# Sketched linear attention and a SwiGLU layer: per-head sums carried to every quadrant by on-chip copies, and a bank counter set

## The chip, the cores and the metric

The kernel runs on one core of a Trainium2 chip. Times are device microseconds. The time before is 309.65 us, the median of three runs (309.54 to 311.03); the profiled execution has a span of 307.8 us from its first to its last instruction. TensorE is called PE here, its weight loads PEld, VectorE DVE, ScalarE ACT, GpSimd POOL, and SP is the engine whose queue issues most of the transfers.

## The reference

Two layers follow each other. All of it is float32 in the kernel; the inputs arrive as 64-bit floats, and the weights are narrowed on the chip.

```python
def phi(x):                                   # x: batch 4, heads 4, tokens 1088, 32
    a = einsum('rd,bhsd->bhsr', S1, x)        # r = 8 sketches
    b = einsum('rd,bhsd->bhsr', S2, x)
    return einsum('bhsi,bhsj->bhsij', a, b)   # 64 features
q_p, k_p = phi(q), phi(k)
kv  = einsum('bhsf,bhsd->bhfd', k_p, v)       # 64 x 32 for each head
z   = sum(k_p, axis=s)                        # 64 for each head
num = einsum('bhsf,bhfd->bhsd', q_p, kv)
den = einsum('bhsf,bhf->bhs', q_p, z) + 1e-06
x   = (num / den) as (4352 tokens, 128)
g   = x @ w_gate                              # 128 -> 1536
out = (silu(g) * (x @ w_val)) @ w_out         # 1536 -> 128
```

## The kernel before, in words

The 4352 tokens are four batches of 1088. A batch is cut into three blocks of 384, 384 and 320 tokens. A **unit** (`unit`, L633) is one block with one of the 12 slices of 128 hidden columns: a matmul with `wg`, one with `wv` (both at L641), a Silu on ACT (L647), and a product on DVE into `hj` (L657). A **down** (`down`, L665) is the matmul of one such `hj` with `wo` into the block's accumulator (L671), run two units later. So for each block and slice PE does three wide matmuls, and these are most of the work. Each fp32 matmul leaves two records in the trace.

The first batch's attention runs by itself at the start, with its own scheme (L755 to L836). The attention of batches 1 to 3 is a generator (`attention`, L476): after every unit from the eighteenth (`z >= 17`) of the first batch on, the loop calls `next(att)` once, and the generator emits a few instructions and yields. What lies between two yields is therefore queued on the engines between two units. [...] a long DVE instruction of the generator stands in front of the next `hj`.

The steps of the generator for one batch are: transposes of K and Q (four steps); the sketches of all tokens, `key_products` for K and again for Q (L278, 18 matmuls each, weights of 128 x 64, into the wide PSUM tiles `a` and `b`); the K features `phk` on DVE; the sum of `phk` over its chunks on POOL (`feature_sums`, L465, tile `zs`); two empty steps; then `kvz`: `key_values` (L312, 36 matmuls of 128 x 32 weights) and the ones-matmul (L523, 128 x 128 weights, 256 columns) that sums `zs` over the partitions and spreads it to all of them; ACT copies `kvs` and `zrep` out (L527, L531); one step later two matmuls with the identity (L537) turn `kvs` to the other layout, and ACT copies it to `kvr` (L542). After that DVE forms `phq` (L553), reduces it (L560), divides (L569 to L575), forms the Q features and transposes them (L301, L584), and 32 matmuls of 32 x 32 (L597) give the numerators, which ACT and DVE copy to `xT` (L614).

The kernel uses eight banks of PSUM. The wide tiles `a` and `b` take four; `g0`, `g1`, `g2` and `acc` are single banks. `bank()` without a name takes `free_banks[turn[0] % len(free_banks)]` and adds one to the counter. In the first 17 units of the main list four banks rotate. At `z == 17` `acc` is taken out of the rotation, because the downs begin and need it, and three rotate from then on (L854). `down` takes `g0` by name for the accumulator of block 1 and `acc` for every other one (L670). `turn[0]` is set to 2 at L816; from there one unit and four more before the loop, and 17 in it, take two banks each, so the counter stands at 2 + 10 + 34 = 46 at `z == 17`.

Of the kernel before, what the change touches and what calls it, by code (L numbers as in the profile page):

```python
# [19 lines left out]
def kernel(  # L20
# [73 lines left out]
    def wide(tag):  # L94
        return psum.tile([P, 2, TB], FP32, tag=tag, name=tag)
# [70 lines left out]

    rebias = const.tile([P, 1], FP32, name="rebias")
    ident = const.tile([P, P], FP32, name="ident")
    ones = const.tile([P, P], FP32, name="ones")
    own = const.tile([P, H], FP32, name="own")  # L170
    sel = const.tile([P, Dh], FP32, name="sel")
    warm = nc.const_aps.tensor(1.0, [P, TB], mybir.dt.bfloat16)
# [83 lines left out]

    xT = const.tile([P, NT], FP32, name="xT")

    s12 = const.tile([P, H, 2, R], FP32, name="s12")
    sq = const.tile([P, 2, R, R], FP32, name="sq")  # L260
    def turn_k(c0, c1):
        four = "p (a c) d -> p a c d"
# [8 lines left out]
            in_=qld[:, 2 * x0 : 2 * x0 + 2 * n, :],  # L271
        )

    def key_products(ps, c0, c1, src=kT):

        for c in range(c0, c1):
            for a in (0, 2):
                nc.tensor.matmul(  # L278
                    ps[32 * a : 32 * a + 64, 64 * (c - c0) : 64 * (c - c0) + 64],
                    src[:, c, a : a + 2, :].rearrange("p a t -> p (a t)"),  # L280
                    s12[:].rearrange("p h t r -> p (h t r)"),
                    start=True,
                    stop=True,
                )
# [13 lines left out]
    def key_features(phk, prod, c0, c1, engine=nc.vector):  # L298
        ka, kb = prod
        n = (c1 - c0) * H  # L300
        engine.tensor_tensor(  # L301
            out=phk[:, c0:c1, :, :, :].rearrange("p c h i j -> p (c h) i j"),
            in0=ka.unsqueeze(3).to_broadcast([P, n, R, R]),
            in1=kb.unsqueeze(2).to_broadcast([P, n, R, R]),
            op=ALU.mult,
        )
# [13 lines left out]
    def unit_sums(kz, phk, c0, c1, order):  # L320

        for c in range(c0, c1):
            a = c % 4
            same = [x for x in order if x % 4 == a]
            nc.tensor.matmul(  # L325
                kz[32 * a : 32 * a + 32, 0 : H * F],
                ones[:, 0:Dh],
                phk[:, c, :, :, :].rearrange("p h i j -> p (h i j)"),
                start=(c == same[0]),
                stop=(c == same[-1]),  # L330
            )
# [144 lines left out]
    def attention(b, qsteps):  # L476
# [13 lines left out]
                load_q(b + 1)  # L490
            yield
        kp, qp = wide("a"), wide("b")
        for ps, src in ((kp, kT), (qp, qT[:].rearrange("p (c a) t -> p c a t", a=4))):
            for i, c in enumerate(kpieces):
                key_products(ps[:, i, :], *c, src=src)
        ka = apool.tile([P, NC * H, R], FP32, tag="kas", name="kas")
        qab = apool.tile([P, 2, NC * H, R], FP32, tag="qab", name="qab")

# [7 lines left out]
        for n, (i, c0, c1) in enumerate(((0, 0, 3), (0, 3, 5), (1, 5, 7), (1, 7, 9))):  # L506
# [10 lines left out]
        zs = feature_sums(phk)  # L517
        yield
        yield
        yield  # L520
        kvz = wide("a")
        key_values(kvz[:, 0, :], phk, 0, NC)
        nc.tensor.matmul(kvz[:, 1, 0 : H * F], ones[:], zs, start=True, stop=True)  # L523

        kvs = apool.tile([P, 2, 4, 32], FP32, tag="kvs", name="kvs")
        zrep = apool.tile([P, H * R, R], FP32, tag="zrep", name="zrep")
        nc.scalar.copy(  # L527
            kvs[:],
            kvz[:, 0, 0:F].rearrange("p (g f) -> p g f", g=2).unsqueeze(2).to_broadcast([P, 2, 4, 32]),
        )  # L530
        nc.scalar.copy(zrep[:], kvz[:, 1, 0 : H * F].rearrange("p (x r) -> p x r", r=R))  # L531
        if b + 1 < B:
            load_v(b + 1, [nc.sync] * 4)
        yield
        kvp = wide("b")[:, 0, 0 : 2 * P].rearrange("p (g n) -> p g n", g=2)
        for g in range(2):
            nc.tensor.matmul(  # L537
                kvp[:, g, :], kvs[:, g, :, :].rearrange("p a f -> p (a f)"), ident[:],
                start=True, stop=True,
            )  # L540
        kvr = apool.tile([P, 2, P], FP32, tag="kvr", name="kvr")
        nc.scalar.copy(kvr[:], kvp)  # L542
        phq = apool.tile([P, NC, H, R, R], FP32, tag="phqs", name="phq")
        phT = apool.tile([P, H, 2, NC, 32], FP32, tag="phk", name="phT")
        dot = apool.tile([P, NC * H, R], FP32, tag="dot", name="dot")
# [1 line left out]
        for s0, s1 in qsteps:  # L547
            thirds = [c for c in fpieces if s0 <= c[0] < s1]
            for c0, c1 in thirds:
                n, x = c1 - c0, slice(H * c0, H * c1)  # L550
                prod = phq[:, c0:c1, :, :, :].rearrange("p c h i j -> p c (h i) j")
                fac = qab[:, 0, x, :].rearrange("p (c h) i -> p c (h i)", h=H)
                nc.vector.tensor_tensor(  # L553
                    out=prod,
                    in0=zrep[:].unsqueeze(1).to_broadcast([P, n, H * R, R]),
                    in1=fac.unsqueeze(3).to_broadcast([P, n, H * R, R]),
                    op=ALU.mult,
                )
                yield
                nc.vector.tensor_reduce(  # L560
                    out=dot[:, x, :],
                    in_=phq[:, c0:c1, :, :, :].rearrange("p c h i j -> p (c h) j i"),
                    axis=AX.X,
                    op=ALU.add,
                )
                yield
            x = slice(H * s0, H * s1)
            w = H * (s1 - s0)
            nc.vector.tensor_tensor(  # L569
                out=dot[:, x, :], in0=dot[:, x, :], in1=qab[:, 1, x, :], op=ALU.mult  # L570
            )
            nc.vector.tensor_reduce(out=den[:, x], in_=dot[:, x, :], axis=AX.X, op=ALU.add)
            nc.vector.tensor_scalar_add(den[:, x], den[:, x], 1e-6)
            nc.vector.reciprocal(den[:, x], den[:, x])
            nc.vector.tensor_tensor(  # L575
                out=qab[:, 0, x, :], in0=qab[:, 0, x, :],
                in1=den[:, x].unsqueeze(2).to_broadcast([P, w, R]), op=ALU.mult,
            )
            yield
            for c0, c1 in thirds:  # L580
                x = slice(H * c0, H * c1)
                key_features(phq, (qab[:, 0, x, :], qab[:, 1, x, :]), c0, c1)
                yield
                nc.vector.transpose(  # L584
                    out=phT[:, :, :, c0:c1, :].rearrange("p h g c t -> p c (h g) t"),
                    in_=phq[:, c0:c1, :, :, :].rearrange(
                        "p c h (g i) j -> p c (h g) (i j)", g=2
                    ),
                )
                yield  # L590
            num = wide("a"), wide("b")
            for g in range(2):
                for h in range(H):
                    for a in range(4):
                        r = slice(32 * a, 32 * a + 32)
                        n = min(s1, (NX - a + 3) // 4) - s0
                        nc.tensor.matmul(  # L597
                            num[a // 2][32 * h : 32 * h + 32, a % 2, 0 : 32 * n],
                            kvr[r, g, 32 * h : 32 * h + 32],
                            phT[r, h, g, s0 : s0 + n, :],  # L600
                            start=(g == 0),
                            stop=(g == 1),
                        )
            for u, engine in enumerate((nc.scalar.copy, nc.vector.tensor_copy)):
                for c0, c1 in query_runs(s0, s1):
                    if c1 == NC and u == 1:
                        continue
                    t0 = S * b + P * c0
                    wd = 4 if c1 < NC else 2
                    dst = xT[:, t0 : t0 + 32 * wd * (c1 - c0)].rearrange(  # L610
                        "p (c a t) -> p a c t", a=wd, t=32
                    )
                    src = num[u][:, :, 32 * (c0 - s0) : 32 * (c1 - s0)]
                    engine(  # L614
                        dst[:, 2 * u : 2 * u + 2], src.rearrange("p a (c t) -> p a c t", t=32)
                    )
            yield
# [111 lines left out]
    for h in range(H):  # L729
# [9 lines left out]
    keep_warm(7, 32, ps=ps)  # L739
    sTv = srep[:, 0 : 2 * R].rearrange("p (t r) -> p t r", t=2)  # L740
    nc.vector.tensor_tensor(
        out=s12[:],
        in0=sTv.unsqueeze(1).to_broadcast([P, H, 2, R]),
        in1=own[:].unsqueeze(2).unsqueeze(3).to_broadcast([P, H, 2, R]),
        op=ALU.mult,
# [22 lines left out]
    phk = apool.tile([P, NC, H, R, R], FP32, tag="phk", name="phk")  # L768
    kz = bank("g0")[:, 0 : H * F]
    key_features(phk, prods[aside], *aside, engine=nc.gpsimd)  # L770
    for c in (c0, c1):
        key_features(phk, prods[c], *c)
    for c in (c0, aside, c1):
# [79 lines left out]
    for z, (i, j) in enumerate(seq):  # L853
        if z == 17:  # L854
            free_banks.pop()
        unit(i, j)
        for p in parts.get(z, ()):
            part(*p)
        if z in (24, 25, 26):
            catch_up()  # L860
        if z == 6:
            load_k(1)
            load_v(1, [nc.sync] * 4)
            load_q(1)
        if z >= 17:
            todo.remove(order[0])
            todo.insert(0, order.pop(0))
            down()
        if z >= 17:
            next(att)  # L870
# [63 lines left out]
```

## Time and profile before

| what | before |
|---|---|
| time, median of 3 | 309.65 us |
| span of the profiled execution | 307.8 us |
| granted PE clock | 1.000 |
| PE busy | 300.5 us |
| DVE, ACT, POOL busy | 173.9, 96.1, 37.2 us |
| L641 and L671, share of the chain that ended last | 57% and 28% |
| L597, L523, L537, share of that chain | about 1% each, or less |

In a timeline of one engine each row gives the start in the span, the duration of the row, the engine, line, operation and tiles, and the number of records that the row merges. A bracket at the end gives idle time of the engine just before the row, and what ended it. The end of a matmul is modelled and reaches beyond the start of the next one, so costs on PE are read from one start to the next, and not from durations.

### The profile page before, as it was taken

How to read it: one execution, taken by the hardware profiler on the slowest of the kernel's cores; microseconds unless marked ns; L12 is line 12 of the kernel's file. 1: busy time of each engine (PE TensorE's matmuls, PEld its weight loads, DVE VectorE, ACT ScalarE, POOL GpSimd, SP SyncE). 2: the span in 40 equal slices, each digit the busy share in tenths (PEclk: the TensorE clock that was granted, in tenths of full speed). 3: DMA queues.
4: the chain of work that ended last, by engine and by line, in shares of the span. 5: the costliest groups of instructions: out<-in, count | busy, mean ns of one | idle time of the engine just before them, and what ended most of it. 6: DMA issues, size and time to landing. Idle time of an engine off the chain costs nothing.

```text
span 307.8 us, 5127 instructions
## 1 busy us (share of the span) xinstructions
PE 300.5 (98%) x2056; PEld 191.2 (62%) x2056; DVE 173.9 (57%) x330; ACT 96.1 (31%) x225; POOL 37.2 (12%) x54
## 2 busy tenths in 40 slices
PE   8899999999999999999999999999999999999995
PEld 6545565657565566666666656555676556676664
DVE  4997887664659546279934552897532323333321
ACT  3566763422003223222232222322222222222230
POOL 3126222174000003300000042000000000000000
PEclk9999999999999999999999999999999999999999
DMA  7554490402111040210100100100000100100101
GB/s 196 167 170 104 146 276 0 147 0 78 23 28 21 2 145 2 51 51 0 26 2 0 22 3 0 28 0 0 14 14 0 21 2 1 26 0 1 23 0 26
DMA packets 24695, 13.96 MB, mean 45 GB/s; under 512 B 18400, under 2 KB 22752, under 8 KB 24672
## 3 DMA queue, kind: packets, MB, share of 16 engines
q1 hardware_dynamic: 24016, 13.54, 17.4%
q8 instruction: 16, 0.26, 0.3%
q10 hardware_dynamic: 656, 0.10, 0.2%
q14 instruction: 7, 0.06, 0.1%
HBM read 11.41 MB, written 2.23 MB: 44 GB/s over the span
## 4 chain that ended last, share of the span: by engine, by line
PE 95%; DVE 2%; DMA 1%; issue 0%; ACT 0%; SPq 0%; DVEq 0%
PE bank L641 57%; PE bank L671 28%; DMA kld<-in_k_dram 1%; PE a L597 1%; PE a L278 1%; PE a L312 1%; PE b L278 1%; PE a L685 1%; PE a L523 1%; PE bank L325 0%; PE bank L278 0%; PE b L537 0%; PE a L369 0%; PE a L421 0%; DVE man L229 0%; PE bank L312 0%
## 5 line engine op out<-in xcount | busy, mean ns | idle before, releaser
L657 DVE TENSOR_TENSOR hj<-sg,bank 128x384 f32<-128x384 f32 (+1 forms) x138 | 73.0, 529 | 104.2 <-PE bank L641 103.7
L647 ACT ACTIVATE sg<-bank 128x384 f32<-128x384 f32 (+1 forms) x144 | 68.0, 473 | 157.4 <-PE bank L641 155.6
L641 PE MATMUL bank<-xT,wg 128*128 128x384 f32 (+1 forms) x288 | 112.7, 473 | 0.8 <-DVE hj L657 0.7
L641 PE MATMUL bank<-xT,wv 128*128 128x384 f32 (+1 forms) x288 | 111.6, 469 | 0.3 <-DVE wv L238 0.2
L671 PE MATMUL bank<-hj,wo 128*128 128x384 f32 (+2 forms) x288 | 105.1, 460 | 0.0
L641 PEld LDWEIGHTS bank<-xT,wv 128*128 128x128 f32 x288 | 54.4, 190 | 34.1 <-DVE hj L657 0.9
L671 PEld LDWEIGHTS bank<-hj,wo 128*128 128x128 f32 x288 | 54.5, 190 | 32.0 <-DVE o L699 0.2
L641 PEld LDWEIGHTS bank<-xT,wg 128*128 128x128 f32 x288 | 53.2, 190 | 32.3 <-DVE hj L657 2.3
L469 POOL TENSOR_TENSOR zs<-phk 128x1024 f32<-128x1024 f32 x3 | 7.0, 2349 | 103.6 <-PE bank L641 103.3
L560 DVE TENSOR_REDUCE dot<-phq 128x96 f32<-128x768 f32 x9 | 13.8, 1531 | 0.0
L301 DVE TENSOR_TENSOR phk<-kas,a 128x512 f32<-128x512 f32 (+1 forms) x12 | 8.7, 749 | 5.2 <-ACT kas L504 5.2
L699 DVE STREAM_TRANSPOSE o<-bank 128x384 f32<-128x384 f32 (+2 forms) x12 | 6.6, 548 | 6.7 <-PE bank L671 6.3
L222 ACT ACTIVATE exp<-exp,rebias 128x384 int32<-128x384 int32 (+3 forms) x15 | 8.3, 551 | 2.3 <-DVE exp L217 1.7
L584 DVE STREAM_TRANSPOSE phT<-phq 128x768 f32<-128x768 f32 x9 | 8.7, 967 | 0.1
L301 DVE TENSOR_TENSOR phq<-qab 128x768 f32<-128x768 f32 x9 | 8.5, 949 | 0.0
L553 DVE TENSOR_TENSOR phq<-zrep,qab 128x768 f32<-128x768 f32 x9 | 8.5, 943 | 0.0
L229 DVE SCALAR_TENSOR_TENSOR man<-raw,man 128x384 f32<-128x384 uint32 (+2 forms) x14 | 7.2, 511 | 0.0
L614 ACT COPY xT<-a 128x64 f32<-128x64 f32 (+3 forms) x7 | 2.3, 367 | 15.6 <-PE b L597 9.2
L225 DVE SCALAR_TENSOR_TENSOR exp<-raw,exp 128x384 int32<-128x384 int32 (+2 forms) x14 | 7.1, 507 | 0.0
L223 ACT ACTIVATE man<-man 128x384 f32<-128x384 int32 (+3 forms) x15 | 6.8, 451 | 0.0
L263 DVE STREAM_TRANSPOSE kT<-kld 128x384 f32<-128x384 f32 (+2 forms) x9 | 6.1, 693 | 0.3 <-DMA kld<-in_k_dram 0.3
L238 POOL TENSOR_TENSOR wo<-man,exp 128x384 f32<-128x384 f32 x4 | 4.1, 1019 | 17.3 <-DVE man L229 17.3
(112 smaller groups left out, 161.2 us busy)
## 6 DMA issues: line engine op xcount, KB each, us to landing
kld<-in_k_dram SPq DMA_DIRECT2D x4, 544.0 KB, 4.1
vld<-in_v_dram SPq DMA_DIRECT2D x12, 144.0 KB, 5.3
qld<-in_q_dram SPq DMA_DIRECT2D x3, 544.0 KB, 3.7
raw<-in_moe_w_out_dram SPq DMA_DIRECT2D x4, 384.0 KB, 3.9
out_dram<-o SPq DMA_DIRECT2D x28, 48.0 KB, 1.8
raw<-in_moe_w_gate_dram SPq DMA_DIRECT2D x3, 384.0 KB, 3.5
raw<-in_moe_w_val_dram SPq DMA_DIRECT2D x3, 384.0 KB, 3.7
out_dram<-o SPq DMA_DIRECT2D x16, 40.0 KB, 1.7
```

The lines of the kernel that those rows point to most:

```text
L222: nc.scalar.activation(e[:], e[:], AF.Relu, bias=rebias[: shape[0], :], scale=8.0)
L225: nc.vector.scalar_tensor_tensor(out=e[:], in0=hi, scalar=-(1 << 31), in1=e[:], op0=ALU.bitwise_and, op1=ALU.bitwise_or,)
L229: nc.vector.scalar_tensor_tensor(out=f, in0=lo, scalar=2.0**-52, in1=f, op0=ALU.mult, op1=ALU.add)
L301: engine.tensor_tensor(out=phk[:, c0:c1, :, :, :].rearrange("p c h i j -> p (c h) i j"), in0=ka.unsqueeze(3).to_broadcast([P, n, R, R]), i ...
L469: add = lambda o, a, b: nc.gpsimd.tensor_tensor(out=o, in0=a, in1=b, op=ALU.add)
L553: nc.vector.tensor_tensor(out=prod, in0=zrep[:].unsqueeze(1).to_broadcast([P, n, H * R, R]), in1=fac.unsqueeze(3).to_broadcast([P, n, H * ...
L560: nc.vector.tensor_reduce(out=dot[:, x, :], in_=phq[:, c0:c1, :, :, :].rearrange("p c h i j -> p (c h) j i"), axis=AX.X, op=ALU.add,)
L584: nc.vector.transpose(out=phT[:, :, :, c0:c1, :].rearrange("p h g c t -> p c (h g) t"), in_=phq[:, c0:c1, :, :, :].rearrange("p c h (g i) ...
L641: nc.tensor.matmul(o[:, 0:n], w[:, j, :], xT[:, t0 : t0 + n], start=True, stop=True)
L647: nc.scalar.activation(sg[:, 0:n], g[:, 0:n], AF.Silu)
L657: nc.vector.tensor_tensor(out=hj[:, 0:n], in0=sg[:, 0:n], in1=u[:, 0:n], op=ALU.mult)
L671: nc.tensor.matmul(acc[i][:, 0:n], wo[:, j, :], hidden[i, j][:, 0:n], start=(j == 0), stop=(j == NCH - 1),)
```

## The change

For batches 1 to 3 the change does away with the two full-width products on sums. It rotates the order of the heads of the Q sketches: in partition quadrant a the slots hold heads a, a+1, a+2, a+3 (modulo 4). For that, `s12` is doubled in width (a POOL copy in the first batch), and each quadrant has its own matmul with its own window of `s12` (`query_sketches`). The sums of each head are then made in that head's own quadrant only, four narrow matmuls in place of one full one. One ACT copy and one DVE transpose put sums and `kv` into slot 0 of a tile `spread`, and for each of three other slots two SBUF-to-SBUF transfers on the SP queue shift it by whole quadrants. The identity product and its copy go. The `kvz` step comes one yield earlier, and four yields stand between it and the first user of `spread`, so the part after it starts two calls later. The product L553 writes its result with i innermost, so that the reduction reads neighbouring elements. The numerator matmuls run in rotated order. Apart from all this, `turn[0] %= 4` is added where the rotation goes from four banks to three.

```diff
-    s12 = const.tile([P, H, 2, R], FP32, name="s12")
+    s12 = const.tile([P, 2 * H, 2, R], FP32, name="s12")
...
+    def query_sketches(ps, c0, c1):
+        for c in range(c0, c1):
+            for a in range(4):
+                nc.tensor.matmul(
+                    ps[32 * a : 32 * a + 32, 64 * (c - c0) : 64 * (c - c0) + 64],
+                    qT[:, 4 * c + a, :],
+                    s12[:, a : a + H, :, :].rearrange("p h t r -> p (h t r)"),
...
-        for ps, src in ((kp, kT), (qp, qT[:].rearrange("p (c a) t -> p c a t", a=4))):
+        for ps, products in ((kp, key_products), (qp, query_sketches)):
...
         zs = feature_sums(phk)
         yield
         yield
-        yield
         kvz = wide("a")
         key_values(kvz[:, 0, :], phk, 0, NC)
-        nc.tensor.matmul(kvz[:, 1, 0 : H * F], ones[:], zs, start=True, stop=True)
-        kvs = apool.tile([P, 2, 4, 32], FP32, tag="kvs", name="kvs")
-        zrep = apool.tile([P, H * R, R], FP32, tag="zrep", name="zrep")
+        for h in range(H):
+            nc.tensor.matmul(
+                kvz[32 * h : 32 * h + 32, 1, 0:F], ones[:], zs[:, F * h : F * h + F],
+                start=True, stop=True,
+            )
+        spread = apool.tile([P, H, 2, F], FP32, tag="spread", name="spread")
         nc.scalar.copy(
-            kvs[:],
-            kvz[:, 0, 0:F].rearrange("p (g f) -> p g f", g=2).unsqueeze(2).to_broadcast([P, 2, 4, 32]),
-        )
-        nc.scalar.copy(zrep[:], kvz[:, 1, 0 : H * F].rearrange("p (x r) -> p x r", r=R))
+            spread[:, 0, 0, :].rearrange("p (j i) -> p j i", j=R),
+            kvz[:, 1, 0:F].rearrange("p (i j) -> p j i", j=R),
+        )
+        nc.vector.transpose(
+            out=spread[:, 0, 1, :].rearrange("p (g d) -> p g d", g=2),
+            in_=kvz[:, 0, 0:F].rearrange("p (g f) -> p g f", g=2),
+        )
+        for s in range(1, H):
+            m = P - 32 * s
+            nc.sync.dma_start(out=spread[0:m, s, :, :], in_=spread[P - m : P, 0, :, :])
+            nc.sync.dma_start(out=spread[m:P, s, :, :], in_=spread[0 : P - m, 0, :, :])
         if b + 1 < B:
             load_v(b + 1, [nc.sync] * 4)
-        yield
-        kvp = wide("b")[:, 0, 0 : 2 * P].rearrange("p (g n) -> p g n", g=2)
-        for g in range(2):
-            nc.tensor.matmul(
-                kvp[:, g, :], kvs[:, g, :, :].rearrange("p a f -> p (a f)"), ident[:],
-                start=True, stop=True,
-            )
-        kvr = apool.tile([P, 2, P], FP32, tag="kvr", name="kvr")
-        nc.scalar.copy(kvr[:], kvp)
+        for _ in range(4):
+            yield
...
                 nc.vector.tensor_reduce(
                     out=dot[:, x, :],
-                    in_=phq[:, c0:c1, :, :, :].rearrange("p c h i j -> p (c h) j i"),
+                    in_=phq[:, c0:c1, :, :, :].rearrange("p c h j i -> p (c h) j i"),
...
-                for h in range(H):
+                for s in range(H):
                     for a in range(4):
                         r = slice(32 * a, 32 * a + 32)
+                        h = (a + s) % 4
...
-                            kvr[r, g, 32 * h : 32 * h + 32],
-                            phT[r, h, g, s0 : s0 + n, :],
+                            kvr[r, s, g, :],
+                            phT[r, s, g, s0 : s0 + n, :],
...
+    nc.gpsimd.tensor_copy(s12[:, H:, :, :], s12[:, 0:H, :, :])
...
         if z == 17:
             free_banks.pop()
+            turn[0] %= 4
         unit(i, j)
```

## The prediction on record

> **What bounds the kernel now.** I read the page first: busy time by engine and the chain of work that ended last.
>
> ```profile
> PE 300.5 (98%) x2056; PEld 191.2 (62%) x2056; DVE 173.9 (57%) x330; ACT 96.1 (31%) x225; POOL 37.2 (12%) x54
> ...
> PE 95%; DVE 2%; DMA 1%; issue 0%; ACT 0%; SPq 0%; DVEq 0%
> ```
>
> PE holds the chain for 95% of the span at a granted clock of 1.000. So an edit is worth what it takes from PE's queue, or what stalls it adds there. Next I read the timeline of PE around the attention steps of batch 2, from start to start.
>
> ```profile
> 112.83 0.81 PE L671 MATMUL bank<-hj,wo 128*128 128x384 f32 x2
> 113.57 1.27 PE L278 MATMUL a<-s,kT 128*64 128x64 f32 x36
> 114.67 1.22 PE L278 MATMUL b<-s,qT 128*64 128x64 f32 x36
> 115.82 0.91 PE L641 MATMUL bank<-xT,wg 128*128 128x384 f32 x2
> ...
> 126.89 0.81 PE L671 MATMUL bank<-hj,wo 128*128 128x384 f32 x2
> 127.63 1.21 PE L312 MATMUL a<-phk,vld 128*32 128x64 f32 x72
> 128.77 0.70 PE L523 MATMUL a<-zs,ones 128*128 128x256 f32 x2
> 129.31 0.81 PE L641 MATMUL bank<-xT,wg 128*128 128x384 f32 x2
> ...
> 131.24 0.61 PE L537 MATMUL b<-ident,kvs 128*128 128x128 f32 x4
> 131.69 0.81 PE L641 MATMUL bank<-xT,wg 128*128 128x384 f32 x2
> ```
>
> A wide matmul of 384 columns takes 0.645 us from start to start. Into L278 and L312 it is 0.74, so a change of the weights' shape costs 0.10; the first wide matmul after the sketches also takes about 0.1 more. The Q sketches hold PE for 1.15, L312 for 1.14, L523 for 0.54 and L537 for 0.45. Batches 1 and 3 show the same lengths within 0.01. Then the timelines of PE and DVE where the rotation of banks changes, and where block 1's accumulator begins:
>
> ```profile
> 46.98 0.81 PE L641 MATMUL bank<-xT,wv 128*128 128x384 f32 x2
> 48.50 0.91 PE L641 MATMUL bank<-xT,wg 128*128 128x384 f32 x2 [0.71 <-DVE hj L657]
> 49.25 0.81 PE L641 MATMUL bank<-xT,wv 128*128 128x384 f32 x2
> ...
> 75.96 0.70 PE L641 MATMUL bank<-xT,wv 128*128 128x320 f32 x2
> 76.50 8.44 PE L671 MATMUL bank<-hj,wo 128*128 128x384 f32 x26
> ```
>
> At z = 17 PE stands still until DVE has read the bank that the unit before has just filled. At z = 29 block 1's accumulator starts without a pause. Last, the end of the sums on POOL, in batch 1 and batch 2 (POOL's timeline):
>
> ```profile
> 70.05 0.72 POOL L469 TENSOR_TENSOR zs<-zs,phk 128x256 f32<-128x256 f32 x1
> ...
> 125.29 0.73 POOL L469 TENSOR_TENSOR zs<-zs,phk 128x256 f32<-128x256 f32 x1
> ```
>
> And what a small transfer on SP's queue takes (the page's list of DMA issues: KB each, us to landing):
>
> ```profile
> out_dram<-o SPq DMA_DIRECT2D x28, 48.0 KB, 1.8
> ```
>
> **What the Trainium skill says.** TensorEngine Tiling (Array Packing), Key Properties: a change of the tiling mode drains TensorE. The 0.10 us above agrees. FP8 and Floating Point Precision, TensorE Precision Notes: true fp32 takes four passes. 384 columns in 0.645 us, against 320 in 0.54, agree with a cost in proportion to the columns. TensorE: Matmul & The Clock Gate, Part 3, says that narrow weights in different column groups run at the same time: L312's 72 records of 64 columns take 1.14/72 = 0.016 us each, while L523's two of 256 columns take 0.27. DMA: Bandwidth & Descriptors, Issuing engines are not separate DMA queues: transfers run on the same 16 engines and interleave. In the trace four stores on SP are issued within 1.90 us, each landing after 1.8.
>
> **The change part by part.**
>
> Q sketches: 36 records of 64-wide weights become 72 of 32-wide ones. That is L312's form and count, so 1.14, plus one more change of shape (64 to 32) at 0.10: 1.24 in place of 1.15, **+0.09 a batch**. Bounds: -0.05 if the change of shape hides, +0.25 if it costs twice as much and narrow loads lag.
>
> Sums: L523's 0.54 goes. Four matmuls of 64 columns are 8 records at 0.016, 0.13, in the shape that L312 left. The return to wide weights, about 0.11, was within L523's 0.54 and now falls on the next unit. 0.24 for 0.54: **-0.30 a batch**. The identity product goes: **-0.45 a batch**. Together -0.66, three batches, **-1.98 us**.
>
> Waits that this adds or moves. The sums matmul comes a unit earlier. In batch 1, PE would reach it 1.08 + 0.645 before its present 72.72, at 71.0; POOL ends at 70.77, 0.2 us ahead, and its start follows PE's own sketches, so that distance stays. In batch 2 it would be 128.77 - 1.94 = 126.83 against 126.02. No stall, though batch 1 is close. Behind the sums in PE's queue stand the next unit and down, for which nobody waits at once.
>
> The copies out: one ACT copy of 64 columns (0.21, as L795) for L527 and L531 (0.37 each) and L542 (0.38); one DVE transpose of 64 columns, which I put at 0.2 from L741's 0.22 for that size. Both run while the next unit's matmuls do: zero. The six transfers wait on SP for both; behind them stand the loads of V, not needed before the next batch's `kvz`, and stores. From the start of L312, `spread` slot 0 is ready after about 1.14 + 0.13 + 0.5 = 1.8 us; six issues at 1.90/4 take 2.9, and landing 1.8: 6.5. The first reader, DVE's L553, comes behind the `hj` four units later, after about 1.4 + 4 x 1.94 = 9.1 us. Hidden, with some 2.6 to spare; the least favourable case, each transfer only after the last has landed, is a rival below. The numerators' order: the same 32 matmuls with the same shapes, four row groups in turn as before: zero, bounds -0.2 to +0.2 a batch.
>
> DVE: L560's mean is 1.531 us for 768 elements at a stride of 8; L572, which reads neighbours, takes 0.25 for 96, 0.35 for 192 and 0.45 for 288, so 1.0 ns an element and 0.15 fixed: 0.95 for 768. DVE isn't on the chain, so mostly zero. It shows in one place: at the start of batch 1, where the first two units have no downs, PE's starts at 94.45, 95.20, 96.52 and 97.27 are 0.085 + 0.105 + 0.025 + 0.105 later than 0.645 apart, while DVE has an L560 of 1.51 and the division there. The two-call shift moves the division later and the reduction shortens: **-0.3 us**.
>
> Counter: at z = 17 it stands at 46. 46 modulo 3 is g1, which z = 16 had just filled as its second bank (45 modulo 4). The pause costs 1.52 - 0.645 = 0.87, plus 0.105 on the restart (48.50 to 49.25): 0.98. With 46 modulo 4 = 2 the unit takes g2 and g0, both long read: **-0.98 us**. But each unit takes two banks, so at z = 29 the counter is 2 + 24 = 26, and that unit takes g2 and **g0** (before: 70 and 71, g1 and g2). Right behind it the down of (1, 0) takes g0 by name. It must then wait for that unit's `hj`. In the DVE timeline this `hj` starts 0.81 after the second matmul's start (76.77 against 75.96) and runs 0.49; with 0.06 to PE as at z = 17 that is 1.36, against 0.54 without: 0.82, plus 0.10 for the restart: **+0.92 us**. So the pause moves rather than goes. Behind it stand 23 downs and nothing that DVE waits for.
>
> The POOL copy of `s12` falls between 8.7 and 13.15, where POOL is idle: zero.
>
> Sum: -1.98 - 0.3 - 0.98 + 0.92 = -2.34. 309.65 - 2.34 = **307.3 us**.
>
> **The rivals.** (1) Little is left, about 308.4: narrow sketches at +0.25, a stall of 0.2 on `zs` in batch 1, and the start of batch 1 as slow as before: 3 x (0.25 - 0.75) + 0.2 - 0.06 = -1.4, so 308.3. For it: the rates are taken from another line. Against: the same form and count. (2) More is gained: the pause at z = 29 isn't there, because something orders the accumulator otherwise, or the rotated order lets the numerators overlap better (up to 0.2 in each of four groups): 309.65 - 2.34 - 0.92 = 306.4. Against: the same kind of wait is plain at z = 17. (3) Slower: the six transfers follow one another, 6 x 1.8 = 10.8 us, so `spread` is ready 12.6 after L312's start and L553 waits up to 3.5. The next `hj` stand behind it on DVE, and their banks run out after about a unit. In batches 2 and 3 nearly all of it reaches PE, in batch 1 no unit waits: 2 x 3 - 2.34 = +3.7, so 313.3. For it: no transfer of this kind is in the trace. Against: the stores on the same queue overlap.
>
> **How the numbers follow.** The forecast gets 0.52, rival (1) 0.22, rival (2) 0.15, rival (3) 0.09, and 0.02 is left for the unforeseen. The predicted time is 307.3. The range of 306.2 to 308.9 takes in rivals (1) and (2) and the bounds of the sketches and numerators, and leaves out rival (3) and the tails. Faster by over 0.5% means below 308.1: the forecast and rival (2), and little of rival (1): 0.68. Within 0.5%: most of rival (1), 0.22. Slower: 0.10.
>
> **What would show it.** The PE timeline after: no L537; sketches of 72 narrow records in about 1.15 to 1.25; 8 narrow records for the sums in about 0.13. No pause at z = 17, a new one of about 0.8 before the down after the last unit of the first batch's list, released by DVE's `hj`. The reduction at about 1 us. A wait of L553 for a transfer, or of the sums for POOL, would prove me wrong there; so would a numerator group much longer than the present 1.5 us.

## The result, and the profile after

The changed kernel takes 307.28 us (307.04 to 307.73, four runs) against 309.74 us beside it: a ratio of 0.9914, with a 95% interval of 0.9884 to 0.9943. Six more runs on another occasion gave 307.29 us and 0.9919 (0.9892 to 0.9946). The forecast was 307.3.

In the code after, the unit is L659 (before L641), its product L675 (L657), the down L689 (L671), the K sketches L290, the Q sketches L278, the K-V products L324 (L312), the sums L535 (L523), the first reader of `spread` L570 (L553), the reduction L577 (L560), the numerators L615 (L597).

The page after, busy time and the chain that ended last:

```profile
PE 298.2 (98%) x2170; PEld 189.4 (62%) x2170; DVE 169.4 (55%) x333; ACT 93.7 (31%) x219; POOL 37.2 (12%) x55
...
PE 95%; DVE 2%; DMA 1%; issue 0%; ACT 0%; SPq 0%; DVEq 0%
```

PE still carries 95% of the chain; it is busy for 2.3 us less, and the span is 2.3 us shorter (305.5 for 307.8). PE's timeline after, around the attention steps of batch 2:

```profile
115.80 0.81 PE L689 MATMUL bank<-hj,wo 128*128 128x384 f32 x2
116.54 1.27 PE L290 MATMUL a<-s,kT 128*64 128x64 f32 x36
117.74 1.21 PE L278 MATMUL b<-s,qT 128*32 128x64 f32 x72
118.88 0.91 PE L659 MATMUL bank<-xT,wg 128*128 128x384 f32 x2
...
128.01 0.81 PE L689 MATMUL bank<-hj,wo 128*128 128x384 f32 x2
128.75 1.21 PE L324 MATMUL a<-phk,vld 128*32 128x64 f32 x72
129.78 0.29 PE L535 MATMUL a<-zs,ones 128*32 128x64 f32 x8
130.01 0.91 PE L659 MATMUL bank<-xT,wg 128*128 128x384 f32 x2
130.76 0.81 PE L659 MATMUL bank<-xT,wv 128*128 128x384 f32 x2
```

From the down to the first unit, the sketches take 3.08 us (118.88 less 115.80), 0.09 more than the 2.99 before. From the down to the unit behind the sums it is 2.00 us in place of 2.42; that unit pays 0.10 for the return to wide weights (its second matmul starts 0.75 on instead of 0.645), so the step is 0.31 shorter. The identity product, 0.45, is gone. Now the two places where PE stood still or began to, in PE's timeline after:

```profile
47.13 0.81 PE L659 MATMUL bank<-xT,wv 128*128 128x384 f32 x2
47.78 0.81 PE L659 MATMUL bank<-xT,wg 128*128 128x384 f32 x2
...
74.46 0.70 PE L659 MATMUL bank<-xT,wv 128*128 128x320 f32 x2
75.81 11.78 PE L689 MATMUL bank<-hj,wo 128*128 128x384 f32 x38 [0.65 <-DVE hj L675]
```

At z = 17 the next matmul starts 0.65 us on, without a pause. Behind z = 29 the first down of block 1 starts 1.35 us after the matmul before it (0.54 in the kernel before), and what it waited for is DVE's `hj`.

### The profile page after: what moved, and what is told of

It reads as the page before. It is cut to its first block, busy times and chain, and to the rows that moved or that the text cites. A ratio compares the mean times of both kernels' runs of the same rounds, so it can differ in the third digit from the quotient of the medians.

```text
span 305.5 us, 5386 instructions
## 1 busy us (share of the span) xinstructions
PE 298.2 (98%) x2170; PEld 189.4 (62%) x2170; DVE 169.4 (55%) x333; ACT 93.7 (31%) x219; POOL 37.2 (12%) x55
## 4 chain that ended last, share of the span: by engine, by line
PE 95%; DVE 2%; DMA 1%; issue 0%; ACT 0%; SPq 0%; DVEq 0%
PE bank L659 58%; PE bank L689 28%; DMA kld<-in_k_dram 1%; PE a L615 1%; PE a L290 1%; PE a L324 1%; PE b L278 1%; PE a L703 1%; PE bank L337 0%; PE bank L290 0%; PE a L381 0%; PE a L433 0%; DVE man L229 0%; PE bank L324 0%; PE b L615 0%
## 5 line engine op out<-in xcount | busy, mean ns | idle before, releaser
L675 DVE TENSOR_TENSOR hj<-sg,bank 128x384 f32<-128x384 f32 (+1 forms) x138 | 73.0, 529 | 98.8 <-PE bank L659 98.3
L659 PE MATMUL bank<-xT,wg 128*128 128x384 f32 (+1 forms) x288 | 112.7, 473 | 0.0
L659 PE MATMUL bank<-xT,wv 128*128 128x384 f32 (+1 forms) x288 | 111.6, 469 | 0.3 <-DVE wv L238 0.2
L689 PE MATMUL bank<-hj,wo 128*128 128x384 f32 (+2 forms) x288 | 105.2, 460 | 0.7 <-DVE hj L675 0.7
L659 PEld LDWEIGHTS bank<-xT,wv 128*128 128x128 f32 x288 | 54.4, 190 | 34.1 <-DVE hj L675 0.9
L689 PEld LDWEIGHTS bank<-hj,wo 128*128 128x128 f32 x288 | 54.5, 190 | 33.0 <-DVE hj L675 1.2
L659 PEld LDWEIGHTS bank<-xT,wg 128*128 128x128 f32 x288 | 53.5, 190 | 31.8 <-issue 2.3
L570 DVE TENSOR_TENSOR phq<-spread,qab 128x768 f32<-128x768 f32 x9 | 8.5, 944 | 0.5 <-DMA spread<-spread 0.5
L577 DVE TENSOR_REDUCE dot<-phq 128x96 f32<-128x768 f32 x9 | 8.5, 942 | 0.0
L263 DVE STREAM_TRANSPOSE kT<-kld 128x384 f32<-128x384 f32 (+2 forms) x9 | 6.1, 693 | 0.5 <-DMA kld<-in_k_dram 0.5
L481 POOL TENSOR_TENSOR zs<-zs 128x512 f32<-128x512 f32 (+1 forms) x6 | 6.0, 996 | 0.5
```

The costliest lines, as they stand in the source:

```text
L481: add = lambda o, a, b: nc.gpsimd.tensor_tensor(out=o, in0=a, in1=b, op=ALU.add)
L570: nc.vector.tensor_tensor(out=phq[:, c0:c1, :, :, :], in0=zrep.unsqueeze(1).to_broadcast([P, n, H, R, R]), in1=fac.unsqueeze(3).to_broadca ...
L577: nc.vector.tensor_reduce(out=dot[:, x, :], in_=phq[:, c0:c1, :, :, :].rearrange("p c h j i -> p (c h) j i"), axis=AX.X, op=ALU.add,)
L659: nc.tensor.matmul(o[:, 0:n], w[:, j, :], xT[:, t0 : t0 + n], start=True, stop=True)
L675: nc.vector.tensor_tensor(out=hj[:, 0:n], in0=sg[:, 0:n], in1=u[:, 0:n], op=ALU.mult)
L689: nc.tensor.matmul(acc[i][:, 0:n], wo[:, j, :], hidden[i, j][:, 0:n], start=(j == 0), stop=(j == NCH - 1),)
```

## The experiments

The medians scatter by up to a microsecond or so, and most of that arises in the head of the kernel: in these profiles the second matmul of z = 16 starts anywhere from 46.8 to 48.7 us. Counted from DVE's first transpose of K (L263), which follows the first load, it starts after 41.56 to 41.60 us in nine of the thirteen profiles. In the other four (counter with g1, changed without counter, narrow Q alone, contiguous reduction alone) it starts after 42.76 to 43.10 us, and there PE's first 36 matmul records on K last 2.19 us in place of 1.40. The first load, landing at different times, shifts the head by up to 0.6 us besides. No edit accounts for this, and why PE begins more slowly in those four is not shown.

So for each run I give, beside its time, its **PE path**: the time from that matmul to the start of the last stretch of PE's final matmuls, read from one profile of each run. The ends of the two paths, in PE's timeline before and after:

```profile
302.00 1.95 PE L685 MATMUL a<-wo,hj 128*128 128x128 f32 x16
...
299.75 1.95 PE L703 MATMUL a<-wo,hj 128*128 128x128 f32 x16
```

The path is 302.00 - 46.98 = 255.02 us before and 299.75 - 47.13 = 252.62 after, a difference of -2.40. How far it repeats is seen from two pairs of profiles: 252.62 and 252.61 for the changed kernel, 251.69 and 251.70 for the changed kernel with the accumulator in `g1`.

| run | time, us | ratio to before (95%) | PE path, us | difference, us |
|---|---|---|---|---|
| counter alone | 310.32 | 1.0001 (0.9987 to 1.0016) | 254.94 | -0.08 to before |
| counter, accumulator in g1 | 309.02 | 0.9973 (0.9960 to 0.9987) | 254.02 | -1.00 to before |
| changed, without counter | 307.94 | 0.9927 (0.9900 to 0.9954) | 252.68 | +0.06 to changed |
| changed, accumulator in g1 | 306.98 | 0.9899 (0.9873 to 0.9924) | 251.69 | -0.93 to changed |
| narrow Q sketches alone | 310.61 | 0.9996 (0.9959 to 1.0032) | 255.29 | +0.27 to before |
| contiguous reduction alone | 309.41 | 0.9968 (0.9934 to 1.0001) | 254.70 | -0.32 to before |
| changed, one empty step | 316.01 | 1.0175 (1.0142 to 1.0208) | 261.08 | +8.46 to changed |
| changed, identity product back | 308.77 | 0.9943 (0.9912 to 0.9974) | 253.95 | +1.33 to changed |
| changed, again | 307.29 | 0.9919 (0.9892 to 0.9946) | 252.61 | -0.01 to changed |
| changed, accumulator in g1, again | 306.26 | 0.9880 (0.9860 to 0.9900) | 251.70 | -0.92 to changed |
| the same with narrow K sketches | 305.83 | 0.9876 (0.9853 to 0.9899) | 251.11 | -1.51 to changed |

### Does the counter take a pause away, or move it?

The counter line alone, on the kernel before:

```diff
         if z == 17:
             free_banks.pop()
+            turn[0] %= 4
```

> The kernel before with the counter line alone. Theory (the pause only moves from z = 17 to the accumulator of block 1 behind z = 29): -0.98 + 0.92 = -0.06 us against before, so about 309.7; PE starts its matmul at z = 17 without a gap, and the first down of block 1 starts about 1.36 us after the matmul before it in place of 0.54. Rival (the counter is set right and a pause is gone): -0.98 us, about 308.8, and no pause at either place.

PE's timeline of this run at the two places:

```profile
46.84 0.81 PE L641 MATMUL bank<-xT,wv 128*128 128x384 f32 x2
47.48 0.81 PE L641 MATMUL bank<-xT,wg 128*128 128x384 f32 x2
...
74.84 0.70 PE L641 MATMUL bank<-xT,wv 128*128 128x320 f32 x2
76.19 1.24 PE L671 MATMUL bank<-hj,wo 128*128 128x384 f32 x3 [0.65 <-DVE hj L657]
```

No pause at the first, 1.35 us from start to start at the second: it has moved. The ratio is 1.0001, and the PE path -0.08 us where -0.06 was expected.

To show that the bank taken by name is what the second one waits for, the same with another bank:

```diff
+            turn[0] %= 4
...
-            acc[i] = bank("g0" if i == 1 else "acc")
+            acc[i] = bank("g1" if i == 1 else "acc")
```

> The kernel before with the counter line, and block 1's accumulator in g1 instead of g0. At z = 29 the unit takes g2 and g0, and g1 was read for the last time by the product of z = 28. Theory: both pauses are gone, -0.98 us against before, about 308.8. Rival (the bank by name isn't what the second pause waits for): as the counter line alone, about 309.7.

PE's timeline of this run, behind z = 29:

```profile
76.62 0.70 PE L641 MATMUL bank<-xT,wv 128*128 128x320 f32 x2
77.15 1.13 PE L671 MATMUL bank<-hj,wo 128*128 128x384 f32 x3
```

0.53 us from start to start, no wait. The PE path is 1.00 us shorter than before, and the ratio of 0.9973 lies clear of 1. So the counter is worth about 1 us, but only together with the other bank.

The other half, the changed kernel without the counter line:

```diff
             free_banks.pop()
-            turn[0] %= 4
```

> The changed kernel without the counter line, so the attention part alone. Theory: nearly all of the gain is the attention part; +0.06 us against the changed kernel, about 307.3 to 307.4, with the pause at z = 17 back and none behind z = 29. Rival (the counter carries 1 us of the gain): about 308.3.

PE's timeline of this run at z = 17:

```profile
48.15 0.81 PE L659 MATMUL bank<-xT,wv 128*128 128x384 f32 x2
49.67 0.91 PE L659 MATMUL bank<-xT,wg 128*128 128x384 f32 x2 [0.71 <-DVE hj L675]
```

The old pause is back, the new one gone (behind z = 29 the down starts 0.54 us on), and the PE path differs by 0.06 us. By the PE path the whole gain is that of the attention part. The median, 307.94 us, lies between forecast and rival and can't decide: its six runs reach from 307.05 to 308.88, and the profiled one has the longer head.

Last, the changed kernel with the accumulator in `g1`, twice:

> The changed kernel with block 1's accumulator in g1 instead of g0. Theory: the pause of 0.82 us and the 0.1 us of the restart behind z = 29 go, nothing else moves: 307.3 - 0.92 = 306.4. Rival (the time is given back, because in the changed kernel the DVE chain behind these downs, and not PE, sets when batch 1 starts): 307.2 to 307.3.

> The changed kernel with block 1's accumulator in g1, once more beside it. Theory: 0.9 us under the changed kernel, by the pause behind z = 29. Rival (only noise): the same.

-0.93 and -0.92 us on the PE path; beside the changed kernel in the second round the medians are 306.26 and 307.29. The rival, that something else would give the time back, is out.

### What the narrow Q sketches cost

```diff
+    def query_sketches(ps, c0, c1):
+        for c in range(c0, c1):
+            for a in range(4):
+                nc.tensor.matmul(
+                    ps[32 * a : 32 * a + 32, 64 * (c - c0) : 64 * (c - c0) + 64],
+                    qT[:, 4 * c + a, :],
+                    s12[:].rearrange("p h t r -> p (h t r)"),
...
-        for ps, src in ((kp, kT), (qp, qT[:].rearrange("p (c a) t -> p c a t", a=4))):
+        for ps, products in ((kp, key_products), (qp, query_sketches)):
```

> The kernel before with the Q sketches as 36 matmuls of 32-wide weights in place of 18 of 64-wide ones, heads not rotated. Theory: one more change of shape, +0.09 us a batch on PE, +0.27 in all, about 310.1. Rival (narrow loads lag or the change of shape costs more): +0.25 a batch, 310.6; rival (narrow weights are faster by themselves): at or under 309.7.

PE's timeline of this run, batch 2:

```profile
115.12 1.27 PE L290 MATMUL a<-s,kT 128*64 128x64 f32 x36
116.31 1.21 PE L278 MATMUL b<-s,qT 128*32 128x64 f32 x72
117.46 0.91 PE L653 MATMUL bank<-xT,wg 128*128 128x384 f32 x2
```

K's part now lasts 1.19 from start to start in place of 1.10, with a change to narrower weights behind it; Q's is 1.15 as before. The PE path is +0.27 us, three times the 0.09 of the working. The time itself (310.61 against 310.84 beside it, a ratio of 0.9996 with an interval of 0.9959 to 1.0032) can't tell so little.

### Whether the reduction's length is what the start of batch 1 lost

```diff
-        nc.scalar.copy(zrep[:], kvz[:, 1, 0 : H * F].rearrange("p (x r) -> p x r", r=R))
+        nc.scalar.copy(
+            zrep[:].rearrange("p (h j) i -> p h j i", h=H),
+            kvz[:, 1, 0 : H * F].rearrange("p (h i j) -> p h j i", h=H, i=R),
+        )
...
-                    in_=phq[:, c0:c1, :, :, :].rearrange("p c h i j -> p (c h) j i"),
+                    in_=phq[:, c0:c1, :, :, :].rearrange("p c h j i -> p (c h) j i"),
```

> The kernel before with the product L553 written with i innermost (the ACT copy of zrep turned to fit), so that the reduction reads neighbours. Theory: the reduction takes 0.95 us in place of 1.53, and the loss of 0.32 us on PE at the start of batch 1 goes, or most of it: about 309.4. Rival (that loss comes from the place of the division in the order and not from the reduction's length): 309.7, the loss still there.

The group of the reduction (mean of one: 942 ns, before 1531), from this run's page:

```profile
L563 DVE TENSOR_REDUCE dot<-phq 128x96 f32<-128x768 f32 x9 | 8.5, 942 | 0.0
```

PE's timeline of this run at the start of batch 1:

```profile
95.43 0.81 PE L644 MATMUL bank<-xT,wv 128*128 128x384 f32 x2
96.07 0.81 PE L644 MATMUL bank<-xT,wg 128*128 128x384 f32 x2
96.72 0.81 PE L644 MATMUL bank<-xT,wv 128*128 128x384 f32 x2
97.36 0.81 PE L674 MATMUL bank<-hj,wo 128*128 128x384 f32 x2
```

All starts are 0.64 to 0.65 apart: the loss is gone, and the PE path is 0.32 us shorter, as worked out. An engine with 57% of busy time had cost PE time here: from 92.4 to 100.1 us of the profile before, DVE has no idle time. The product itself kept its mean of 943 ns, so what got shorter is the reduction; the later place of the division wasn't needed for it. The medians, 309.41 against 310.84, are further apart than the PE paths because of the head; the lowest runs of the two, 309.38 and 309.79, are 0.41 apart.

### The identity product by itself

```diff
+        yield
+        kvp = wide("b")[:, 0, 0 : 2 * P].rearrange("p (g n) -> p g n", g=2)
+        for g in range(2):
+            nc.tensor.matmul(
+                kvp[:, g, :], ident[:], ident[:], start=True, stop=True,
+            )
+        kvd = apool.tile([P, 2, P], FP32, tag="kvd", name="kvd")
+        nc.scalar.copy(kvd[:], kvp)
-        for _ in range(4):
+        for _ in range(3):
             yield
```

> The changed kernel with two identity products of the old shape (128 x 128 weights, 128 columns) put back a step after the K-V products, as dead work: their result is copied and not used. Theory (PE time is paid one to one, and the product's absence is the largest term): +0.45 us a batch, +1.35 in all, 308.6. Rival (the gain comes from elsewhere, and such a product fits into slack): 307.3 to 307.6.

PE's timeline of this run, batch 2:

```profile
131.94 0.81 PE L697 MATMUL bank<-hj,wo 128*128 128x384 f32 x2
132.58 0.61 PE L560 MATMUL b<-ident 128*128 128x128 f32 x4
133.03 0.81 PE L667 MATMUL bank<-xT,wg 128*128 128x384 f32 x2
```

0.45 us from start to start, +1.33 us on the PE path for three batches, 308.77 us. What PE is given to do in this stretch is paid one to one.

### What the four empty steps hide

```diff
-        for _ in range(4):
+        for _ in range(1):
             yield
```

> The changed kernel with one empty step in place of four between the transfers and their first reader. Theory (the transfers take about 7.1 us from the start of the K-V products to the last landing, and only the four steps hide them): DVE waits about 3.7 us for a transfer in each batch; PE loses about 1.5 us in batches 2 and 3 and 3.2 us more behind z = 29 in batch 1, where the accumulator waits for a product queued behind the waiting one: 307.3 + 6.2 = 313.5. Rival (three banks and the lag of the downs cover such a wait): under 308.3.

The direction was right, the size not: +8.46 us on the PE path in place of 6.2. The waits on DVE were close to what was expected. DVE's timeline of this run, batch 1:

```profile
76.22 0.96 DVE L570 TENSOR_TENSOR phq<-spread,qab 128x768 f32<-128x768 f32 x1 [3.92 <-DMA spread<-spread]
```

And PE's, in batch 1 behind z = 29, and in batch 2:

```profile
74.44 0.70 PE L659 MATMUL bank<-xT,wv 128*128 128x320 f32 x2
79.36 8.16 PE L689 MATMUL bank<-hj,wo 128*128 128x384 f32 x20 [4.21 <-DVE hj L675]
...
134.79 0.81 PE L689 MATMUL bank<-hj,wo 128*128 128x384 f32 x2
136.78 0.91 PE L659 MATMUL bank<-xT,wg 128*128 128x384 f32 x2 [1.19 <-DVE hj L675]
```

Behind z = 29 PE's pause grows from 1.35 to 4.92 us from start to start, +3.57. In batch 2 the start is 1.99 us on for 0.645, and the restart costs 0.10: 1.45. Batch 3 has 1.69 in the same way, and the start of batch 1 loses 0.33 again, because here the division stands in front of that block's first `hj`. Together 7.0; 1.4 us were left. The granted clock accounts for them, as the stretches of this run show (length, busy us and count of PE, PEld, DVE, ACT and POOL, then the granted PE clock, the share of the DMA engines and GB/s):

```profile
78.00:79.30 1.30, 0.00 (x0) 0.00 (x0) 1.30 (x4) 0.00 (x0) 0.00 (x0) 0.84 0.47 86
79.30:80.00 0.70, 0.64 (x1) 0.50 (x2) 0.60 (x5) 0.00 (x0) 0.00 (x0) 0.50 0.54 81
80.00:82.00 2.00, 2.00 (x4) 1.01 (x3) 1.47 (x4) 0.00 (x0) 0.00 (x0) 0.50 0.33 49
82.00:84.00 2.00, 2.00 (x7) 1.26 (x6) 0.95 (x1) 0.00 (x0) 0.00 (x0) 0.92 0.02 4
```

In this pause the granted clock falls to half, 0.50 (the mean of 0.84 in the first stretch puts the fall at 78.9, some 3.9 us after PE's last work ended), and it stays there until about 82.3 (from the mean of 0.92 in the last). Some 2.9 us of work at half speed lose about 1.45. Checked against the downs: ten of them, 6.45 us, lie between 79.36 and the numerators, which start at 87.45 and not at 79.36 + 6.45 + 0.09 (shape) + 0.10 (restart) = 86.00: 1.45 late. So the run says two things: the transfers do take some 7 us to be ready, and this pause cost more than its length.

### A version that beats both

The K sketches have their own change of shape to the Q sketches, now that those are narrow. On the changed kernel with the accumulator in `g1`:

```diff
-            acc[i] = bank("g0" if i == 1 else "acc")
+            acc[i] = bank("g1" if i == 1 else "acc")
...
+    def key_sketches(ps, c0, c1):
+        for c in range(c0, c1):
+            for a in range(4):
+                nc.tensor.matmul(
+                    ps[32 * a : 32 * a + 32, 64 * (c - c0) : 64 * (c - c0) + 64],
+                    kT[:, c, a, :],
+                    s12[:, 0:H, :, :].rearrange("p h t r -> p (h t r)"),
...
-        for ps, products in ((kp, key_products), (qp, query_sketches)):
+        for ps, products in ((kp, key_sketches), (qp, query_sketches)):
```

> The changed kernel once more, beside the two that follow, on one chip: 0.9923 of before by the step sum (309.65 - 2.40 by the traces).

> The changed kernel with block 1's accumulator in g1, and the K sketches of batches 1 to 3 as 36 matmuls of 32-wide weights too, so that no change of shape lies between the K and the Q sketches. Theory (a change of shape costs 0.10 us, and 72 narrow records of 64 columns take 1.03): K's part 1.20 to 1.03, -0.17 a batch, -0.5 in all, 0.5 us under the same kernel with wide K. Rival (both widths run at the same rate and the change of shape is only moved to the front): no gain.

PE's timeline of this version, batch 2:

```profile
115.49 1.21 PE L290 MATMUL a<-s,kT 128*32 128x64 f32 x72
116.52 1.19 PE L278 MATMUL b<-s,qT 128*32 128x64 f32 x72
117.64 0.91 PE L671 MATMUL bank<-xT,wg 128*128 128x384 f32 x2
```

K's part falls from 1.20 to 1.03, and Q's from 1.14 to 1.12. The PE path is 251.11 us, 0.59 under the same kernel with wide K sketches. The median is 305.83 us, against 306.26 for that, 307.29 for the changed kernel and 309.73 before, all side by side: a ratio to before of 0.9876 (0.9853 to 0.9899). It is the fastest of the runs; that it is faster than the kernel with wide K sketches rests on the PE path, since the two intervals overlap.

## Why the prediction was right, point by point

**What bounds the kernel.** Right: the identity product put back costs 1.33 us for the 1.35 that PE spends on it.

**The sum.** -1.98 - 0.3 - 0.98 + 0.92 = -2.34 was forecast; the PE path moved by -2.40 and the median by -2.46. The terms add up to that too: narrow Q sketches +0.27 (by themselves), identity product -1.33 (put back), sums 3 x -0.31 = -0.93 (read from the traces only), reduction -0.32 (by itself), counter -0.08 (by itself): -2.39. So no large error in one term was made good by another; inside the term of the sums two small ones were.

**Q sketches, +0.09 a batch.** Right, 0.09 from start to start, and three times that in the run of their own.

**Sums, -0.30.** Right in size, though the parts were split wrongly. L312's 1.14 us were taken as the bare products, but held the change to L523's shape as well: with the sums in the same shape they take 1.03. The 0.23 of the sums, put at 0.13, then contains the change back. Two errors of 0.1 us cancel here, which is luck. They also make the margin on POOL smaller than the 0.2 us forecast for batch 1. POOL's timeline after:

```profile
69.33 0.73 POOL L481 TENSOR_TENSOR zs<-zs,phk 128x256 f32<-128x256 f32 x1
```

It ends about 70.06; PE's sums start at 70.15 in that batch. No stall, by 0.1 us.

**The counter.** Right: the pause has moved from z = 17 to the accumulator of block 1. Forecast 1.36 us from start to start, measured 1.35.

**The transfers.** Hidden, as forecast, but with less to spare. The SP queue's timeline after, the first and the last of batch 2's six:

```profile
130.67 0.54 SPq L553 DMA_DIRECT2D spread<-spread  x1
...
133.80 0.59 SPq L554 DMA_DIRECT2D spread<-spread  x1
```

They are issued 0.63 us apart, not 0.48 as the stores suggested, and land after 1.9 us each. From the start of L324 (128.75) the last lands after some 7.0 us in place of 6.5; in batch 2 the reader comes at 137.95, 9.2 us after it, where 9.1 was forecast. In batch 1 DVE reaches L570 sooner and does wait, in the DVE timeline after:

```profile
76.25 0.96 DVE L570 TENSOR_TENSOR phq<-spread,qab 128x768 f32<-128x768 f32 x1 [0.49 <-DMA spread<-spread]
```

At that point no `hj` stands behind it, only downs run on PE, and nobody pays. The forecast had said that such a wait would prove it wrong there; it did so for the claim that DVE would not wait, and not for the cost. The rival in which the transfers follow one another is out: they overlap.

**DVE.** The reduction was put at 0.95 and takes 0.94; the loss at the start of batch 1 is gone, and the reduction alone is enough for that.

**The numerators.** Zero, from the traces only: 1.50 us from their start to the next unit in both kernels (154.91 to 156.41 before, 159.79 to 161.29 after). The order wasn't tried by itself, and neither was the POOL copy of `s12`; but of the nine profiles whose heads agree, two are without the copy (41.60 and 41.58 us) and seven with it (41.56 to 41.58), so it cost nothing there, as forecast.

**The rivals.** Rival (2) named the right place for more gain, and it could be had: the accumulator in another bank is worth 0.92 us. But it isn't what the change does.

## What to carry to other kernels

Where one engine carries the whole chain, cost an edit from start to start on that engine, shape changes and restarts included; here the sum then held to a tenth of a microsecond. When a rotation of buffers is put in order, follow the counter to its end, and to every place that takes one of the same buffers by name: a pause may only have moved there. And for a transfer to be hidden, count what is queued behind its reader: in batch 1 of the changed kernel DVE waits 0.49 us and PE loses nothing, since no product stands behind the reader; in the run with one empty step DVE waits 11.3 us in all, and with a product behind each reader PE lost between 1.45 and 3.57 us in each batch.

## What the runs showed of the hardware that was not expected

PE's clock fell to 0.50 in a pause of 4.2 us and stayed there for some 2.9 us of work, which cost about 1.45 us on top; after the same run's pauses of 1.19 and 1.42 us it was 1.00. The Trainium skill, TensorE: Matmul & The Clock Gate, Part 1, says that an idle window of about 3.4 us takes PE back to half its rate; this case agrees, though no run here has a pause between 1.42 and 4.2 us. In four of the thirteen profiles PE's first matmuls on K took 2.19 us for 36 records in place of 1.40, while the granted clock on record reads 1.00; the same form takes 1.10 later. SBUF-to-SBUF transfers of 16 to 48 KB were issued 0.63 us apart on one queue and landed after 1.8 to 2.0 us whatever their size. And 72 narrow matmul records of 64 columns (1.03 us) go faster than 36 of double width (1.10), when no change of shape follows them.
